# Decode attention with a cached window: V loaded and summed one quarter behind K, without filler matmuls in the loop

## The chip, the cores and the metric

The kernel runs on one core of one Trainium2 chip. The metric is the device time of one execution in microseconds (us). Three runs of the kernel before gave 291.79, 292.34 and 293.69; their median, 292.34, is the time before. A profiled execution, taken by the hardware profiler, is the source of every row quoted.

The engines are named as the profile names them: PE does the matmuls (PEld its weight loads), DVE is the vector engine, ACT the scalar engine, POOL GpSimd, and SP the engine whose queue issues nearly all DMAs.

## What is computed

One decode step of a transformer block for a batch of two, all in bfloat16:

```
h  = x + Attention(layernorm(x))        # 32 heads of 192, the last 2048 of 8192 cached tokens
h2 = h + (gelu(n @ w_gate) * (n @ w_up)) @ w_down      # n = layernorm(h)

q = (layernorm(x) @ wq)                               # x: 2 x 1 x 640
scores = q . k[window] * 192**-0.5                    # k_cache, v_cache: 2 x 32 x 8192 x 192
o = softmax(scores) . v[window];  attention = o @ wo
```

There is one query token for each of the two batch entries, so K and V are each read once and used once. They are 50 MB each (2 x 32 x 2048 x 192 x 2 bytes); with wq, wo and the three matrices of the feed-forward part it is 122 MB.

## The kernel before

**Tiles.** For each batch entry the window of 2048 tokens is cut into four *quarters* of 512 tokens. A quarter's K is one tile of 128 partitions (32 heads times 4 runs of 128 tokens) by 49152 bytes, 6.29 MB, loaded by one DMA; V likewise. So there are eight quarters, K0 to K7 and V0 to V7; quarters 0 to 3 are batch entry 0. Each quarter is worked in two *groups* `g` of 64 tokens per partition, so there are 16 groups.

**The ring.** All large loads go to one SBUF tensor, `ring`, which has three places of 49152 bytes. K tiles alternate between the first and the second (`K_AT`); V has the third alone (`V_AT`). `wq` at the start lies over the second and part of the third. After the attention, the three first parts of `wo` take the first place, the fourth part, `w_gate` and `w_up` the second, and `w_down` the third. `load` puts each DMA into a list in program order; `pump` (L358 to 374) issues from the head of that list for as long as what the next load overwrites has been marked `done`. The list is in order: a load that must wait holds back all behind it. SP issues them, and each waits there on the semaphores of the last instructions that read the place. K is marked done by its last transpose (L559), V by the second of its sums (L671).

The list is: `wq`, then K0, V0, K1, V1 to K7, V7, then four parts of `wo`, `w_gate`, two parts of `w_up`, four parts of `w_down`. A small first part of `w_gate` has a place of its own.

**One group.** `transposes(g)` (L558): 48 transposes on PE of K, seen as pairs of bfloat16 in one 4-byte word, into four half banks of PSUM, `tps`, 12 times four; each four are copied to `ktr`, 7 times by DVE (L569) and 5 times by ACT (L567). `scores(g)` (L616): 24 matmuls into the bank `sps`. `softmax(g)`: DVE masks, finds the minimum of the negated scores (L627), ACT takes the exponent into `eexp` (L631). `e_blocks(g)`: DVE transposes `eexp` into `et` (L655) and copies it in four parts (L657) into `eblk[g % 2]`, whose blocks are the weights for V. `pv(g)` (L669): 64 matmuls that sum V, weighted, into the bank `ops_` for even `g` and `m1` for odd; DVE copies the result to `osb` (L679) for three groups out of four.

**A pair of quarters.** Four groups are one turn of the loop (`J`, four turns), and the running maximum and sums are carried on once a turn: `maxima()` (DVE, ACT), `sums()` (PE, DVE, ACT), `combine()` (two pairs of small matmuls L683 and L684, then DVE: `osum` is scaled and the four partial results are added to it, L693). When a batch entry is finished, `heads_done(b)` (PE L704, DVE) arranges `osum` by heads into `ot`; for entry 0 it runs in the turn `J == 2`, for entry 1 after the loop. Then `oproj` (L728) multiplies by `wo`, and the feed-forward part follows, ending with `w_down` (L873), a cast (L879) and the store (L880).

**Fillers.** `keep_busy(n)` (L753) issues `n` matmuls of 512 columns of float32 whose result nobody reads (two instructions each). It is called with 10 ahead of the loop and with 6 after each quarter but the last.

**Order.** Each engine's order is the order in which the program calls `pe`, `dve`, `act`; `_Prog` works out the semaphore waits from what each operation reads and writes (a write to a buffer waits for its earlier readers). PE and DVE have a hardware loop of four turns; pieces that don't run in each turn (`op` for `heads_done(0)`, `fill` for the filler at the end of a turn) stand in `If` blocks, in the order given at L904. The turn of the loop is, for its two quarters:

```
transposes(g, 0, 12); scores(g); softmax(g)
transposes(g + 1, 0, 12); scores(g + 1)
e_blocks(g); softmax(g + 1)
if g % 4 == 2: maxima()
e_blocks(g + 1); pv(g)
if g % 4 == 2: sums()
pv(g + 1)
if g % 4 == 2: combine()
... heads_done(0) in turn 2, keep_busy(6)
```

Of the kernel before, what the change touches and what calls it, by code (L numbers as in the profile page):

```python
# [6 lines left out]
F32 = mybir.dt.float32  # L7
# [9 lines left out]
DH = 192  # L17
# [10 lines left out]
LOOPED = ("pe", "dve")  # L28
BIAS = 16
RARE = ()  # L30

# [24 lines left out]
class _Prog:  # L56
# [17 lines left out]
    def op(self, eng, fn, R=(), W=(), X=(), dma=None, cls=0):  # L74
        if self.seg == "op" and eng in LOOPED:
            cls = 2
        elif eng == "pe" and self.seg in RARE:
            cls = 1
# [161 lines left out]
WQ_AT = SLOT  # L240
WO_AT = (0, 15360, 30720, SLOT)
WG_AT = SLOT + 15360
WU_AT = WG_AT + 12288
WD_AT = (V_AT, V_AT + 7680, V_AT + 7680 + 3840, V_AT + 7680 + 3840 + 2560)


def bass_sequential_preLN__sliding_block_cached__geglu_ffn__decode_kernel(
# [12 lines left out]
    with ExitStack() as ctx:  # L260
# [67 lines left out]
        eblk = sb("eblk", [128, 2, 16, 4, 32], BF16)  # L328
        osb = sb("osb", [128, 4, DH], F32)
        osum = sb("osum", [128, DH], F32)  # L330
# [56 lines left out]
        def load_v(i):  # L387
            load(("v", i), V_AT, SLOT, kv_src(A_v_cache, i), lambda v: v, f"v{i % 2}")

# [49 lines left out]
        for i in range(2 * NQ):  # L439
            load_k(i)  # L440
            load_v(i)
        for J in range(4):
# [198 lines left out]
        def sums():  # L641
# [10 lines left out]
            dve(tt(wz[:, 6:7], wz[:, 5:6], zsum[:, :], ALU.mult), R=["wz5", "zsum"], W=["wz6"], cls=0)  # L652

        def e_blocks(g):
            dve(lambda e: e.transpose(et[:, :], eexp[:, :]), R=["eexp"], W=["et"], cls=0)  # L655
            for hg in range(4):
                dve(lambda e, hg=hg: e.tensor_copy(eblk[32 * hg:32 * (hg + 1), g % 2, :, hg, :],  # L657
                                                   et[32 * hg:32 * (hg + 1), :].rearrange("p (a x) -> p a x", x=32)),
                    R=["et"], W=[("eb", g % 2, hg)], cls=0)

        def pv(g):
# [14 lines left out]
            if g % 2 == 1:  # L676
                done(("v", g // 2))
            if g % 4 != 3:
                dve(lambda e: e.tensor_copy(osb[:, g % 4, :], bank[:, 0:DH]), W=[("osb", g % 4)], X=[x], cls=0)  # L679

        def combine():
            def fn(e):
                e.matmul(m2[:, 264:270], lhsT=rowperm[:, :], rhs=wz[:, 0:6], start=True, stop=True)  # L683
                return e.matmul(m2[:, 270:271], lhsT=rowsum[:, :], rhs=wz[:, 6:7], start=True, stop=True)  # L684

            pe(fn, R=["rowperm", "rowsum", "wz", "wz5", "wz6"], X=["m2"])
            dve(lambda e: e.tensor_copy(wp[:, :], m2[:, 264:270]), W=["wp"], X=["m2"], cls=0)
            dve(lambda e: e.reciprocal(rinv[:, :], m2[:, 270:271]), W=["rinv"], X=["m2"], cls=0)
            dve(tt(wfin[:, :], wp[:, 5:6], rinv[:, :], ALU.mult), R=["wp", "rinv"], W=["wfin"], cls=0)
            dve(ts(osum[:, :], osum[:, :], wp[:, 4:5], ALU.mult), R=["wp", "osum"], W=["osum"], cls=0)  # L690
            for k in range(4):
                src = osb[:, k, :] if k < 3 else m1[:, 0:DH]
                dve(lambda e, k=k, src=src: e.scalar_tensor_tensor(out=osum[:, :], in0=src, scalar=wp[:, k:k + 1], in1=osum[:, :],  # L693
                                                                   op0=ALU.mult, op1=ALU.add),
                    R=["wp", "osum"] + [("osb", k)] * (k < 3), W=["osum"], X=["m1"] * (k == 3), cls=0)

# [53 lines left out]
        def keep_busy(n):  # L750
            def fn(e):
                for k in range(n):
                    ins = e.matmul(tps[3][:, :], lhsT=identf[:, :], rhs=cf[:, :, :].rearrange("p k x -> p (k x)"), start=True, stop=True)  # L753
                return ins

            pe(fn, R=["identf", "cf0", "cfm"], X=[("t", 3)])

# [5 lines left out]
        for J in range(4):  # L763
            P.loop_seg("a", J)
            for g in (4 * J, 4 * J + 2):
# [117 lines left out]

        P.resolve({("dve", 0): 4 * 15 + 14, ("dve", 1): 0, ("dve", 2): 1, ("pe", 2): 1, ("act", 1): 0, ("act", 0): 4 * 6 + 2, ("pool", 0): 4})
        sems = {}
# [7 lines left out]
        P.emit("act", nc.scalar, sems)  # L893
        order = ["a", (1, 3, ["op"]), "b"]
        P.emit_loop("dve", nc.vector, sems, 4, order)
        P.emit_loop("pe", nc.tensor, sems, 4, order + [(None, 3, ["fill"])])

# [27 lines left out]
```

## Time and profile before

| what | value |
|---|---|
| median of three runs | 292.34 us (291.79 to 293.69) |
| the profiled execution's own time | 293.98 us |
| its span, first to last instruction | 292.7 us |
| PE busy | 220.6 us (75%), of it L558 transposes 90.4, L753 filler 50.8, L616 25.1, L669 25.8 |
| DVE busy | 149.6 us (51%) |
| ACT busy | 94.6 us (32%) |
| moved by DMA | 122.44 MB, mean 418 GB/s over the span |
| mean granted TensorE clock | 0.950 |

A row of the timeline gives the start, the length, the engine, the line, the operation and its tiles; SPq is SP's DMA queue. The row PEclk of the page, and the clock column of a windows view, give the clock that TensorE was granted as a share of full speed. Before its first recorded change, at 27.6 us, the clock is printed as 1.00 without having been recorded. Engines run beside each other, so busy times can't be added up; what sets the end is the last wait of each stage.

### The profile page before, as it was taken

What the parts mean: (1) busy time and instruction counts of PE and PEld (TensorE: products, weight loads), DVE (VectorE), ACT (ScalarE), POOL (GpSimd) and SP (SyncE); (2) the same over time, 40 slices, a digit from 0 to 9 for tenths busy, and PEclk for the clock granted to TensorE, in tenths of its full rate; (3) what the DMA queues carried; (4) which work ended last, traced back from release to release, by engine and by line L of the source; (5) the groups of instructions that cost most, each with busy time, mean ns of one, the idle gap of its engine ahead of it and who ended that gap; (6) DMA issues with size and microseconds to landing.
All of it is one profiled execution on the core that took longest, in us unless ns stands there. A gap on an engine that the chain in (4) does not pass through costs nothing.

```text
span 292.7 us, 6397 instructions
## 1 busy us (share of the span) xinstructions
PE 220.6 (75%) x2641; PEld 155.6 (53%) x2641; DVE 149.6 (51%) x369; ACT 94.6 (32%) x128; POOL 23.0 (8%) x69
## 2 busy tenths in 40 slices
PE   2008998597859795879599867988798879874974
PEld 1004476347735773477357646576657647653542
DVE  5000056715684667066834675268556844686431
ACT  1001056306530662066204640166116614550000
POOL 8930200000020000000200000000200000000000
PEclk9999999999999999999959996899799999999596
DMA  8999999999999999999999999999799999999994
GB/s 323 446 462 437 425 430 430 427 419 437 425 430 425 430 430 431 430 430 430 430 430 437 437 437 443 443 430 437 302 430 430 430 430 430 430 395 432 423 411 173
DMA packets 4203, 122.44 MB, mean 418 GB/s; under 512 B 478, under 2 KB 608, under 8 KB 1248
## 3 DMA queue, kind: packets, MB, share of 16 engines
q1 hardware_dynamic: 4188, 122.29, 97.4%
q8 instruction: 7, 0.11, 0.1%
q14 instruction: 4, 0.03, 0.0%
q10 hardware_dynamic: 4, 0.00, 0.0%
HBM read 122.29 MB, written 0.00 MB: 418 GB/s over the span
## 4 chain that ended last, share of the span: by engine, by line
DMA 40%; PE 34%; issue 9%; DVE 9%; ACT 5%; SPq 1%; DVEq 0%
DMA ring<-in_A_k_cache_dram 25%; PE tpp L558 18%; PE tpp L753 9%; DMA ring<-in_B_w_down_dram 8%; DMA ring<-in_A_wq_dram 7%; PE m L669 4%; ACT eexp L631 3%; DVE eblk L657 3%; DVE et L655 3%; PE tpp L578 2%; DVE sm L627 2%; ACT ktr L567 2%; PE sps L704 1%; PE m L683 0%; SPq L374 0%
## 5 line engine op out<-in xcount | busy, mean ns | idle before, releaser
L569 DVE COPY ktr<-tpp 128x1024 bf16<-128x1024 bf16 x112 | 76.7, 691 | 64.0 <-PE tpp L558 62.4
L567 ACT ACTIVATE ktr<-tpp 128x1024 bf16<-128x1024 bf16 x80 | 76.5, 1018 | 92.9 <-PE tpp L558 92.9
L558 PE MATMUL tpp<-identf,ring 128*128 128x128 f32 x768 | 90.4, 276 | 7.1 <-DMA ring<-in_A_k_cache_dram 4.9
L558 PEld LDWEIGHTS tpp<-identf,ring 128*128 128x128 f32 x768 | 83.1, 140 | 20.1 <-DMA ring<-in_A_k_cache_dram 7.6
L753 PE MATMUL tpp<-cf,identf 128*128 128x512 f32 x104 | 50.8, 643 | 0.0
L616 PE MATMUL sps<-ktr,rq 128*32 128x512 bf16 x384 | 25.1, 390 | 13.8 <-DVE ktr L569 13.8
L753 PEld LDWEIGHTS tpp<-cf,identf 128*128 128x128 f32 x104 | 21.1, 208 | 24.1 <-issue 23.6
L669 PE MATMUL m<-ring,eblk 128*32 128x192 bf16 x512 | 13.6, 265 | 17.1 <-DVE eblk L657 17.1
L631 ACT ACTIVATE eexp<-sm,nms 128x512 bf16<-128x512 f32 x16 | 11.6, 723 | 43.2 <-DVE nms L627 43.2
L616 PEld LDWEIGHTS sps<-ktr,rq 128*32 128x32 bf16 x384 | 9.8, 94 | 24.4 <-ACT ktr L567 17.5
L434 POOL TENSOR_TENSOR rq<-qs,mask 128x192 bf16<-128x192 bf16 x16 | 7.8, 517 | 181.8 <-PE sps L616 168.2
L669 PEld LDWEIGHTS m<-ring,eblk 128*32 128x32 bf16 x512 | 11.5, 113 | 18.3 <-DVE eblk L657 18.3
L657 DVE COPY eblk<-et 32x512 bf16<-32x512 bf16 x64 | 18.2, 285 | 2.1
L578 PE MATMUL tpp<-ring,xnT 128*32 128x384 bf16 x80 | 5.9, 482 | 15.3 <-DMA ring<-in_A_wq_dram 15.3
L627 DVE CUSTOM_DVE_ANT_1 sm<-sps,mska 128x512 f32<-128x512 f32 x16 | 11.0, 690 | 9.1 <-issue 8.8
L655 DVE STREAM_TRANSPOSE et<-eexp 128x512 bf16<-128x512 bf16 x16 | 11.3, 706 | 5.0 <-ACT eexp L631 5.0
L669 PEld LDWEIGHTS ops<-ring,eblk 128*32 128x32 bf16 x512 | 10.4, 108 | 6.1 <-DVE eblk L657 6.1
L669 PE MATMUL ops<-ring,eblk 128*32 128x192 bf16 x512 | 12.2, 248 | 1.9 <-DVE eblk L657 1.9
L578 PEld LDWEIGHTS tpp<-ring,xnT 128*32 128x32 bf16 x80 | 3.2, 137 | 17.7 <-issue 15.3
L601 DVE CAST qs<-ops 128x384 bf16<-128x384 f32 x1 | 0.6, 558 | 21.9 <-PE ops L596 21.9
L585 ACT ACTIVATE qrow<-tpp 128x768 bf16<-128x768 f32 x1 | 0.8, 811 | 20.6 <-PE tpp L578 20.6
L704 PE MATMUL sps<-onrm,colsel 128*128 128x192 f32 x8 | 3.0, 524 | 3.7 <-DVE nms L699 3.7
(143 smaller groups left out, 104.7 us busy)
## 6 DMA issues: line engine op xcount, KB each, us to landing
ring<-in_A_k_cache_dram SPq DMA_DIRECT2D x8, 6144.0 KB, 35.5
ring<-in_A_v_cache_dram SPq DMA_DIRECT2D x8, 6144.0 KB, 21.5
ring<-in_A_wq_dram SPq DMA_DIRECT2D x1, 7680.0 KB, 21.2
ring<-in_A_wo_dram SPq DMA_DIRECT2D x4, 1920.0 KB, 24.9
ring<-in_B_w_gate_dram SPq DMA_DIRECT2D x1, 1536.0 KB, 22.0
ring<-in_B_w_up_dram SPq DMA_DIRECT2D x1, 1536.0 KB, 25.3
ring<-in_B_w_down_dram SPq DMA_DIRECT2D x1, 960.0 KB, 21.6
ring<-in_B_w_down_dram SPq DMA_DIRECT2D x1, 480.0 KB, 22.4
```

The lines of the kernel that those rows point to most:

```text
L434: return lambda e: e.tensor_tensor(out=out, in0=a, in1=b, op=op)
L558: ins = e.transpose(bank[:, 128 * u:128 * (u + 1)], kv[:, off:off + 128], identf[:, :])
L567: act(lambda e, dst=dst, src=src: e.activation(out=dst, in_=src, func=ACT.Copy), W=[("kt", n)], X=[x])
L569: dve(lambda e, dst=dst, src=src: e.tensor_copy(dst, src), W=[("kt", n)], X=[x], cls=0)
L578: ins = e.matmul(tps[0][32 * r:32 * (r + 1), 0:384], lhsT=xnT[:, c, 32 * J:32 * (J + 1)], rhs=wq[:, c, 1536 * J + 384 * r:1536 * J + 384 * ...
L616: ins = e.matmul(sps[32 * hg:32 * (hg + 1), :], lhsT=rq[:, k, hg, :], rhs=cols, start=(k == 0), stop=(k == 5), tile_position=(0, 32 * hg))
L627: dve(lambda e: e.tensor_tensor_reduce(out=sm[:, :].rearrange("p (u x) -> p u x", x=32), in0=sps[:, :].rearrange("p (u x) -> p u x", x=32) ...
L631: act(lambda e: e.activation(out=eexp[:, :], in_=sm[:, :], func=ACT.Exp, bias=nms[:, n:n + 1], scale=-1.0, accum_out=zr[:, n:n + 1]), R=[( ...
L655: dve(lambda e: e.transpose(et[:, :], eexp[:, :]), R=["eexp"], W=["et"], cls=0)
L657: dve(lambda e, hg=hg: e.tensor_copy(eblk[32 * hg:32 * (hg + 1), g % 2, :, hg, :], et[32 * hg:32 * (hg + 1), :].rearrange("p (a x) -> p a ...
L669: ins = e.matmul(bank[32 * r:32 * (r + 1), 0:DH], lhsT=eblk[:, g % 2, a, :, :].rearrange("p s x -> p (s x)")[:, r:128:4], rhs=vv[:, DH * t ...
L753: ins = e.matmul(tps[3][:, :], lhsT=identf[:, :], rhs=cf[:, :, :].rearrange("p k x -> p (k x)"), start=True, stop=True)
```

## The change

The diff does five things.

1. In the list of loads, V of a quarter stands behind the next quarter's K: `wq`, K0, K1, V0, K2, V1, ... K7, V6, V7, then the weights in the same order as before.
2. V7 is loaded to the ring's first place, where K6 was. `wo`'s first three parts go to V's place and `w_down` to the first place; the rest stays.
3. The sums over a quarter's V (`pv`) are done in the next quarter, right behind that quarter's scores. For the second quarter of a pair they are in a new function `behind`, together with the scaling of `osum` and the four additions, which now read the last two partial results from PSUM; `combine` keeps the small matmuls and the weights. `behind` runs in an `If` block `pa` in the turns after the first, and once after the loop. For the first quarter of a pair they stand behind `maxima()`.
4. `e_blocks` is split: the transpose of the exponents is `e_turn`, and `e_turn(g)` stays ahead of the next softmax, while the four copies to `eblk` stand behind the sums over the earlier V, whose weights they overwrite.
5. The loop has no filler. The filler ahead of the loop has the same 10 matmuls, of 128 columns.

The diff, cut to its core:

```diff
-RARE = ()
+RARE = ("pa",)
...
-WO_AT = (0, 15360, 30720, SLOT)
+WO_AT = (V_AT, V_AT + 15360, V_AT + 30720, SLOT)
...
-WD_AT = (V_AT, V_AT + 7680, V_AT + 7680 + 3840, V_AT + 7680 + 3840 + 2560)
+WD_AT = (0, 7680, 7680 + 3840, 7680 + 3840 + 2560)
...
-            load(("v", i), V_AT, SLOT, kv_src(A_v_cache, i), lambda v: v, f"v{i % 2}")
+            load(("v", i), V_AT if i < 2 * NQ - 1 else 0, SLOT, kv_src(A_v_cache, i), lambda v: v, f"v{i % 2}")
...
             load_k(i)
-            load_v(i)
+            if i > 0:
+                load_v(i - 1)
+        load_v(2 * NQ - 1)
...
+        def e_turn(g):
+            dve(lambda e: e.transpose(et[:, :], eexp[:, :]), R=["eexp"] + [("eb", 0, 3)] * (g % 2), W=["et"], cls=0)
+
         def e_blocks(g):
-            dve(lambda e: e.transpose(et[:, :], eexp[:, :]), R=["eexp"], W=["et"], cls=0)
...
-            if g % 4 != 3:
+            if g % 4 < 2:
                 dve(lambda e: e.tensor_copy(osb[:, g % 4, :], bank[:, 0:DH]), W=[("osb", g % 4)], X=[x], cls=0)
...
+        def behind(g):
             dve(ts(osum[:, :], osum[:, :], wp[:, 4:5], ALU.mult), R=["wp", "osum"], W=["osum"], cls=0)
             for k in range(4):
-                src = osb[:, k, :] if k < 3 else m1[:, 0:DH]
+                if k == 2:
+                    pv(g)
+                    pv(g + 1)
+                src, tok, x = ((osb[:, 0, :], [("osb", 0)], []), (osb[:, 1, :], [("osb", 1)], []), (ops_[:, 0:DH], [], ["o"]),
+                               (m1[:, 0:DH], [], ["m1"]))[k]
...
-                    ins = e.matmul(tps[3][:, :], lhsT=identf[:, :], rhs=cf[:, :, :].rearrange("p k x -> p (k x)"), start=True, stop=True)
+                    ins = e.matmul(tps[3][:, 0:128], lhsT=identf[:, :], rhs=cf[:, 0, :], start=True, stop=True)
...
-                e_blocks(g)
+                e_turn(g)
                 softmax(g + 1)
-                if g % 4 == 2:
-                    maxima()
-                e_blocks(g + 1)
-                pv(g)
-                if g % 4 == 2:
-                    sums()
-                pv(g + 1)
-                if g % 4 == 2:
-                    combine()
                 if g % 4 == 0:
+                    if J > 0:
+                        P.loop_seg("pa", J)
+                        behind(g - 2)
                     if J == 2:
                         P.loop_seg("op", J)
                         heads_done(0)
+                    P.loop_seg("a2", J)
+                else:
+                    maxima()
+                    pv(g - 2)
+                    pv(g - 1)
+                e_blocks(g)
+                e_turn(g + 1)
+                e_blocks(g + 1)
+                if g % 4 == 0:
                     P.loop_seg("b", J)
-                    keep_busy(6)
-                elif J < 3:
-                    P.loop_seg("fill", J)
-                    keep_busy(6)
+                else:
+                    sums()
+                    combine()
         P.loop_seg()
+        behind(14)
         heads_done(1)
```

More of the change, by code (lines that the diff above doesn't have):

```diff
@@ L76, in op @@
             cls = 2
-        elif eng == "pe" and self.seg in RARE:
+        elif eng in LOOPED and self.seg in RARE:
             cls = 1
@@ L328, in bass_sequential_preLN__sliding_block_cached__geglu_ffn__decode_kernel @@
         eblk = sb("eblk", [128, 2, 16, 4, 32], BF16)
-        osb = sb("osb", [128, 4, DH], F32)
+        osb = sb("osb", [128, 2, DH], F32)
         osum = sb("osum", [128, DH], F32)
@@ L689, in combine @@
             dve(tt(wfin[:, :], wp[:, 5:6], rinv[:, :], ALU.mult), R=["wp", "rinv"], W=["wfin"], cls=0)
+        def behind(g):
             dve(ts(osum[:, :], osum[:, :], wp[:, 4:5], ALU.mult), R=["wp", "osum"], W=["osum"], cls=0)
             for k in range(4):
-                src = osb[:, k, :] if k < 3 else m1[:, 0:DH]
+                if k == 2:
[3 more added lines that the diff above has]
+                               (m1[:, 0:DH], [], ["m1"]))[k]
                 dve(lambda e, k=k, src=src: e.scalar_tensor_tensor(out=osum[:, :], in0=src, scalar=wp[:, k:k + 1], in1=osum[:, :],
                                                                    op0=ALU.mult, op1=ALU.add),
-                    R=["wp", "osum"] + [("osb", k)] * (k < 3), W=["osum"], X=["m1"] * (k == 3), cls=0)
+                    R=["wp", "osum"] + tok, W=["osum"], X=x, cls=0)
         def heads_done(b):
@@ L752, in fn @@
                 for k in range(n):
-                    ins = e.matmul(tps[3][:, :], lhsT=identf[:, :], rhs=cf[:, :, :].rearrange("p k x -> p (k x)"), start=True, stop=True)
+                    ins = e.matmul(tps[3][:, 0:128], lhsT=identf[:, :], rhs=cf[:, 0, :], start=True, stop=True)
                 return ins
-            pe(fn, R=["identf", "cf0", "cfm"], X=[("t", 3)])
+            pe(fn, R=["identf", "cf0"], X=[("t", 3)])
         consts_late()
@@ L881, in bass_sequential_preLN__sliding_block_cached__geglu_ffn__decode_kernel @@
              dma="dout")
-        P.resolve({("dve", 0): 4 * 15 + 14, ("dve", 1): 0, ("dve", 2): 1, ("pe", 2): 1, ("act", 1): 0, ("act", 0): 4 * 6 + 2, ("pool", 0): 4})
+        P.resolve({("dve", 0): 4 * 14 + 12, ("dve", 1): 5, ("dve", 2): 1, ("pe", 2): 1, ("act", 1): 0, ("act", 0): 4 * 6 + 2, ("pool", 0): 4})
         sems = {}
@@ L893, in bass_sequential_preLN__sliding_block_cached__geglu_ffn__decode_kernel @@
         P.emit("act", nc.scalar, sems)
-        order = ["a", (1, 3, ["op"]), "b"]
+        order = ["a", (0, None, ["pa"]), (1, 3, ["op"]), "a2", "b"]
         P.emit_loop("dve", nc.vector, sems, 4, order)
-        P.emit_loop("pe", nc.tensor, sems, 4, order + [(None, 3, ["fill"])])
+        P.emit_loop("pe", nc.tensor, sems, 4, order)
 _INS = ['A_x', 'A_k_cache', 'A_v_cache', 'A_wq', 'A_wo', 'B_x', 'B_w_gate', 'B_w_up', 'B_w_down']
```

## Prediction

> **What bounds the kernel now.** I read first the page's part 2 (40 slices of 7.3 us), because the kernel moves 122 MB:
>
> ```profile
> PEclk9999999999999999999959996899799999999596
> DMA  8999999999999999999999999999799999999994
> GB/s 323 446 462 437 425 430 430 427 419 437 425 430 425 430 430 431 430 430 430 430 430 437 437 437 443 443 430 437 302 430 430 430 430 430 430 395 432 423 411 173
> ```
>
> The transfers are busy in all slices but slice 28 (302 GB/s), the first and the last. So a change of engine work is worth only what it does to holes in this row. Second, the windows view over chosen stretches (columns: length, busy us and count of PE, PEld, DVE, ACT, POOL, granted clock, DMA share, GB/s):
>
> ```profile
> 37.85:125.41 87.56, 69.59 (x859) 49.85 (x858) 48.87 (x111) 33.80 (x44) 1.94 (x4) 1.00 1.00 433
> 125.41:210.50 85.09, 71.19 (x842) 52.96 (x846) 52.83 (x126) 34.28 (x46) 3.89 (x8) 0.91 1.00 430
> 210.50:212.50 2.00, 2.00 (x26) 1.49 (x18) 0.27 (x3) 0.00 (x0) 0.00 (x0) 0.64 0.00 0
> 212.50:256.10 43.60, 37.98 (x399) 27.55 (x398) 25.32 (x52) 18.56 (x24) 0.00 (x0) 1.00 1.01 433
> 256.10:289.78 33.68, 23.30 (x397) 14.98 (x395) 17.05 (x58) 5.40 (x11) 0.00 (x0) 0.86 0.95 398
> ```
>
> One hole of 2.00 us with nothing moved; otherwise 430 to 433 GB/s. The last stretch is the weights. Third, who made the hole: SP's queue in the timeline, which issues each V (first line) with the next K right behind:
>
> ```profile
> 178.18 0.54 SPq L374 DMA_DIRECT2D ring<-in_A_v_cache_dram  x1
> 178.76 0.60 SPq L374 DMA_DIRECT2D ring<-in_A_k_cache_dram  x1
> 211.34 0.53 SPq L374 DMA_DIRECT2D ring<-in_A_v_cache_dram  x1
> 211.92 0.61 SPq L374 DMA_DIRECT2D ring<-in_A_k_cache_dram  x1
> ```
>
> V6 went out only at 211.34, when V5 had been summed; the steps before it were 29 to 31 us, this one 33.2. Data followed 1.2 us later (212.5). Last, why it was late: the clock column, in windows of 3.41 us, on whose grid every recorded change of clock lies.
>
> ```profile
> 85.64:89.05 3.41, 1.36 (x64) 1.30 (x64) 2.73 (x12) 0.46 (x2) 0.15 (x1) 1.00 1.02 437
> 123.19:126.60 3.41, 1.55 (x12) 1.19 (x12) 0.50 (x1) 0.06 (x1) 0.00 (x0) 1.00 0.80 346
> 143.67:147.08 3.41, 1.32 (x64) 1.27 (x64) 2.73 (x12) 0.56 (x3) 0.16 (x1) 1.00 1.00 432
> 147.08:150.49 3.41, 3.41 (x20) 2.06 (x12) 1.89 (x7) 0.00 (x0) 0.00 (x0) 0.50 1.03 447
> 150.49:153.91 3.42, 3.42 (x5) 1.35 (x4) 0.42 (x1) 0.00 (x0) 0.00 (x0) 0.50 0.93 402
> 208.52:211.94 3.42, 3.40 (x68) 3.10 (x68) 0.89 (x7) 0.29 (x1) 0.00 (x0) 0.50 0.33 144
> ```
>
> After a window with PE busy 1.32 us or less the clock is 0.50 for one or two windows; after 1.36 it is not. At half clock the 12 filler matmuls took 8.05 us in place of 5.26 (chain of waits at 148.39 and 212.15), a sum over V 2.76 in place of 1.52. Fillers stand ahead of the next quarter's transposes on PE, so each such stretch delayed the following V.
>
> **The change, part by part.** A quarter is the work on one K tile (6.29 MB) in two groups. Two tiles take 29.06 us (K2 to K3, 96.35 to 125.41). Let T be a K's landing.
>
> *No filler in the loop.* 84 instructions of L753 go, seven groups of 12, at 0.43 us each 36 us of PE; they lie beside transfers, so their removal is worth only the delays above. The price: PE then sits idle from the sum over V to the next K, some 9 us, so at least one window is empty and every quarter begins at half clock. The filler ahead of the loop shrinks from 512 to 128 columns: its 20 instructions, 8.83 us, become 2.3 (at 0.116, a transpose) to 3.8 (at 0.19, its weight load). It ends by 34 and K0 lands at 38.05: quarter 0 starts cold too.
>
> *V one quarter behind.* Landings become K0 38.05, K1 52.6, V0 67.2, K2 81.7, V1, K3 and so on, 14.5 apart; bytes and their total are the same. In quarter 125.41 the scores of both groups end at 141.79, T+16.4, and two sums over V (1.52 each) now follow at once on PE, since V of the quarter before landed at T+14.5: V's place is free at T+19.5. Before, they waited for exponent, transpose and four copies, and V was free at T+22.1 (147.48). It must be free by T+29.1-1.2 = T+27.9 or the transfers run dry. So 5.8 us of room become 8.4, of which the cold start takes its part. How much: the clock came back after one full busy window at 208.52, after two at 147.08; cold lasts 3.4 to 6.8 us and costs half of that, 1.7 to 3.4, 2.6 taken. V free at T+22.1: no hole.
>
> *DVE.* The transpose of the exponents and the four copies are the same 5 instructions per group, split in two functions. Copies to osb (L679, 0.36) fall from 12 to 8: 1.4 us off DVE, off the path. The 16 multiply-adds (0.42) stay; half now read the banks of the sum directly, 0.42 too by the row that reads m. The copies to eblk now wait for the last quarter's sums over V (they reuse its place), and what is queued behind them on DVE are the next quarter's copies out of the transposes. In a first-of-pair quarter: two multiply-adds 0.84, copies 1.24, transpose 0.71, copies 1.24, about 4.1 us after V is free: T+26.2, 2.9 us ahead of the next K. In a second-of-pair quarter PE itself waits for the combine: two osb copies beside PE, then 3.2 us of copies, 1.1 of sums, 1.0 of small matmuls, 5.6 in all, T+27.7. If the room were gone, these would be added to the next quarter. In the quarter of heads_done(0) (5.2 us of DVE, 178.58 to 183.81) DVE is free at 162 + 0.8 + 5.2 + 3.3 = 171.5, K5 lands near 169: quarter 5 starts 1.6 us late (its copies begin 0.7 after its transposes), and its V is free 4 us ahead of need.
>
> *The start is tight.* Quarter 0 has no sum over V: its scores end at 54.82 in the trace, cold 56.4 to 58.2; DVE then does softmax 0.9, copies, transpose, copies, 4.2 in all, before quarter 1's first copy, so quarter 1 behaves as if K1 had landed at 59.9 to 61.7. V0 is summed at 79.4 to 81.2, and up to 3.4 later if PE's wait for DVE cools it again. V1 is wanted at 81.7-1.2 = 80.5: a hole of 0 to 4 us, 0.8 taken, since only the cooled cases reach it. K2 to K7 then have 1.4 us and more.
>
> *Places of the weights.* On SP, wo0 to wo2 now wait for V6's sum (quarter 7, about 250) while V7 runs until 256: no hole. wd waits for V7's sum, 256 + 1 to 6 us, and is wanted after wo, wg and wu, 25 us later: none either. V7 lands where it did; its sum is no longer behind quarter 7's softmax, so the head's tail starts no later. The end is what it was: last wd landed 289.78, then 0.74, 0.33, and the store to 292.7.
>
> *Branches.* One `If` more on DVE, one in place of another on PE. heads_done(0) sits in one: DVE went from 178.55 to 178.58 across it. Between 0 and 0.4 us, beside transfers: nothing.
>
> **Sum**, against the profiled execution's own time, 293.98 (span 292.7 and 1.3 around it): the hole goes, -2.0 by the empty row, -2.9 if the thin share before it (0.33 in its window: 1.1 us of work in the 4.0 from 208.52 to 212.5) counts too; I take -2.6, the fuller account less what skewed engines give back; +0.8 at V1. That is 292.2. The runs shown have a median of 292.34 and a least of 291.79, so they lost less than this execution; on their scale I take **291.9**. Its own range: 291.1 with no hole at all, less 0.3 for scatter, to 294.5 with a V1 hole of 3.5: 290.8 to 294.5.
>
> **Rivals.** *The transposes do not bring the clock back.* No row shows transposes alone doing so: it returned under filler, under q's projection, under sums over V. Half clock doubles filler (0.43 to 0.86) and makes a sum 2.76; by that, 48 transposes 5.57 become about 10.6, 24 scores 1.54 about 2.9. A quarter's scores then end at 2 x (10.6+0.9+2.9) = T+28.8, V free at T+34.3, 6.4 past need, from PE's first cold quarter on; it decides once cold lasts over 16.8 us, twice 8.4. Dense sums warm PE, and it runs on without idling, so every second quarter is spared. Quarter 0 and 1 end at 66.9 and 101.2 against 80.5: 20.7 lost, then 3 x 6.4: 291.9+40 = 332. For it: the first window at 147.08, mostly filler, did not suffice. Against: window 123.19 held only 0.36 of filler and 1.19 of transposes and did not cool where 1.32 of sums did, so transposes count almost fully. The Trainium skill's TensorE: Matmul & The Clock Gate, Part 4: PE-mode transpose, says that the full clock does not engage for transposes, which do not count as busy in the same way; by that rule this rival holds and the sum would be 332, while the trace bears it out only in that nothing shows the reverse.
>
> *It comes back only with the first scores.* Then the first group is cold (T+14.4), the second takes 8.4, V free at T+25.9: no loss in the steady state, but quarter 0 ends at 60.9, quarter 1 acts as from 64.4, and V0 is summed at 83.9 (warm) or 90.3: 3.4 to 9.8 lost, 295.3 to 301.7, say 298.
>
> *Faster.* The weights' stretch, 398 GB/s, might run at 433 with SP's waits moved: 13.4 MB in 30.9 instead of 33.7, so 291.1-2.8 = 288.3. Nothing in the change shortens these rows.
>
> **How the numbers follow.** About 1% is what a measurement can tell from no change: 289.4 to 295.3. Forecast 0.62 at 291.9; first scores 0.20, of which 0.02 stays under 295.3; no return 0.13; faster 0.05. Of the forecast 0.02 lies above 295.3. So faster 0.05, same 0.62, slower 0.33. The range, 290.3 to 302, leaves out the 332 case and the fast one, 0.18.
>
> **What would show it.** Right: slice 28's hole gone; no filler rows in the loop; granted clock 0.50 at each quarter's start and 1.00 within 7 us; SP's V issues 27 us or less after their K landings; sums of 1.52. Wrong: transposes at 0.2 us spacing for a whole group, V issues past T+28, empty DMA windows near 81 and at later tile ends. A change of the 430 GB/s itself would upset the sum altogether.

## The result and the profile after

The changed kernel is slower by 0.7%. The ratio of its runs to those of the kernel before is 1.0067 (95% interval 1.0048 to 1.0086): medians 294.63 us (22 runs, 293.62 to 298.40) and 292.31 (22 runs, 291.79 to 294.58). The time lies in the range given and within the 1% called no change, but 2.7 us above the forecast, and on the other side of the time before. Ratios here are taken over fast runs alone (three of after's 22, near 298, are left out as over 1.5% above its fastest) and are not the quotients of the medians. The profiled execution took 294.99 us with a span of 293.7, against 293.98 and 292.7.

Part 2 of the page of after, the rows that answer to those of before (40 slices of 7.34 us):

```profile
PEclk9999959979977996999599959996997599868555
DMA  8999999999889999999999999999999999999994
GB/s 322 486 425 428 424 428 428 424 418 428 353 321 428 428 430 428 428 428 442 442 455 449 428 428 428 428 442 449 428 428 428 428 428 428 428 389 430 423 416 171
```

The hole of before in slice 28 is gone (428 GB/s). A new one stands in slices 10 and 11 (353 and 321), at 73 to 88 us. The clock row shows a dip in every quarter, and a tail at half clock; 86.4 us of the span are granted half clock, in before 29.5.

SP's queue in the timeline of after, around the new hole and in the next two quarters (V first, then K):

```profile
54.55 0.54 SPq L374 DMA_DIRECT2D ring<-in_A_k_cache_dram  x1
81.34 0.54 SPq L374 DMA_DIRECT2D ring<-in_A_v_cache_dram  x1
81.92 0.60 SPq L374 DMA_DIRECT2D ring<-in_A_k_cache_dram  x1
107.89 0.54 SPq L374 DMA_DIRECT2D ring<-in_A_v_cache_dram  x1
108.47 0.61 SPq L374 DMA_DIRECT2D ring<-in_A_k_cache_dram  x1
135.04 0.54 SPq L374 DMA_DIRECT2D ring<-in_A_v_cache_dram  x1
```

The landings recorded for the issues are K0 37.87, K1 52.42, V0 67.14, K2 81.62, V1 98.86, K3 113.39. All steps are 14.5 to 14.7 us but K2 to V1, which is 17.24: a hole of 2.71. V1 was issued 0.3 us ahead of K2's landing; V2, 5.5 ahead of K3's, and V3, 7.4 ahead of K4's (142.45), left no hole, nor did any later one.

The windows view of after, half a microsecond a row (columns as before: busy PE, PEld, DVE, ACT, POOL, then clock, DMA share, GB/s):

```profile
79.50:80.00 0.50, 0.50 (x36) 0.50 (x29) 0.33 (x2) 0.50 (x1) 0.50 (x2) 1.00 0.01 0
80.00:80.50 0.50, 0.50 (x36) 0.50 (x29) 0.36 (x1) 0.45 (x3) 0.50 (x2) 1.00 0.13 33
80.50:81.00 0.50, 0.50 (x36) 0.50 (x26) 0.00 (x0) 0.00 (x0) 0.21 (x1) 1.00 0.00 0
82.00:82.50 0.50, 0.00 (x0) 0.00 (x0) 0.47 (x2) 0.00 (x0) 0.00 (x0) 1.00 0.00 0
82.50:83.00 0.50, 0.00 (x0) 0.00 (x0) 0.34 (x3) 0.00 (x0) 0.00 (x0) 1.00 2.73 885
```

This view counts a DMA packet whole in the row in which it starts (so the last row can show 2.73), and the packets of a tile are 48 KB and take 1.82 us each. What the rows say is that hardly a packet starts from 79.5 on; those begun before are still moving. Packet by packet, ten of the 16 engines ended their share of K2 between 79.52 and 79.76 and the other six by 81.16, the landing is recorded at 81.62, and V1's first packets started between 82.66 and 84.03, the first of them 1.3 us behind the issue. So the engines run dry and start again one after another. PE is meanwhile in the sums over V0 that V1 waits for. V1 landed 17.52 us behind its issue, V6 of before, in its hole, 17.50, where a tile in the flow takes 14.53. The profile of before, at the issue of V6 (211.34):

```profile
DMA to landing us min/median/max: 17.5/17.5/17.5
```

The difference of the spans is accounted for. The last tile landed at 258.70 for 257.87: 0.97 more of holes (2.88 in all for 1.91) less 0.14 for an earlier K0. The weights behind it took 32.35 us for 32.27, and from the last landing (291.05 for 290.14) to the end it was 2.63 for 2.52. That is 0.83 + 0.08 + 0.11, the 1.02 between the spans.

### The profile page after: what moved, and what is told of

Same layout as the page of the kernel before. It is cut to its first block, busy times and chain, and to the rows that moved or that the text cites. A ratio compares the mean times of both kernels' runs of the same rounds, so it can differ in the third digit from the quotient of the medians.

```text
span 293.7 us, 6215 instructions
## 1 busy us (share of the span) xinstructions
PE 188.1 (64%) x2557; PEld 155.5 (53%) x2557; DVE 148.0 (50%) x365; ACT 95.5 (33%) x128; POOL 23.0 (8%) x69
## 4 chain that ended last, share of the span: by engine, by line
DMA 56%; PE 29%; issue 6%; ACT 3%; DVE 3%; SPq 1%; DVEq 0%
DMA ring<-in_A_k_cache_dram 48%; PE tpp L560 19%; DMA ring<-in_A_wo_dram 9%; PE sps L618 3%; PE m L673 2%; PE ops L673 2%; ACT ktr L569 2%; ACT eexp L633 1%; DVE ktr L571 1%; SPq L374 1%; DVE sm L629 1%; PE sps L837 1%; PE m L886 1%; PE m L738 1%; PE ops L837 1%
## 5 line engine op out<-in xcount | busy, mean ns | idle before, releaser
L560 PE MATMUL tpp<-identf,ring 128*128 128x128 f32 x768 | 107.4, 307 | 36.6 <-DMA ring<-in_A_k_cache_dram 30.5
L560 PEld LDWEIGHTS tpp<-identf,ring 128*128 128x128 f32 x768 | 100.1, 160 | 45.6 <-DMA ring<-in_A_k_cache_dram 31.6
L569 ACT ACTIVATE ktr<-tpp 128x1024 bf16<-128x1024 bf16 x80 | 77.4, 1020 | 75.0 <-PE tpp L560 75.0
L618 PEld LDWEIGHTS sps<-ktr,rq 128*32 128x32 bf16 x384 | 10.3, 94 | 24.0 <-ACT ktr L569 17.5
L661 DVE COPY eblk<-et 32x512 bf16<-32x512 bf16 x64 | 18.2, 284 | 2.0 <-DVE nms L629 0.2
L580 PE MATMUL tpp<-ring,xnT 128*32 128x384 bf16 x80 | 5.3, 443 | 15.3 <-DMA ring<-in_A_wq_dram 15.3
L673 PE MATMUL ops<-ring,eblk 128*32 128x192 bf16 x512 | 13.7, 261 | 2.1 <-DMA ring<-in_A_v_cache_dram 2.1
L673 PEld LDWEIGHTS ops<-ring,eblk 128*32 128x32 bf16 x512 | 12.9, 112 | 3.2 <-DMA ring<-in_A_v_cache_dram 2.2
L687 PE MATMUL m<-wz,rowperm 128*128 128x6 f32 x8 | 2.4, 369 | 17.2 <-DVE wz L434 17.2
L673 PE MATMUL m<-ring,eblk 128*32 128x192 bf16 x512 | 12.7, 249 | 0.0
L580 PEld LDWEIGHTS tpp<-ring,xnT 128*32 128x32 bf16 x80 | 2.9, 127 | 17.4 <-issue 15.4
L687 PEld LDWEIGHTS m<-wz,rowperm 128*128 128x128 f32 x8 | 2.0, 312 | 17.6 <-DVE wz L434 17.6
L738 PE MATMUL m<-ring,ot 128*2 128x320 bf16 x96 | 6.3, 423 | 6.6 <-DMA ring<-in_A_wo_dram 6.6
```

Of the source, the lines that this page charges most:

```text
L560: ins = e.transpose(bank[:, 128 * u:128 * (u + 1)], kv[:, off:off + 128], identf[:, :])
L569: act(lambda e, dst=dst, src=src: e.activation(out=dst, in_=src, func=ACT.Copy), W=[("kt", n)], X=[x])
L580: ins = e.matmul(tps[0][32 * r:32 * (r + 1), 0:384], lhsT=xnT[:, c, 32 * J:32 * (J + 1)], rhs=wq[:, c, 1536 * J + 384 * r:1536 * J + 384 * ...
L618: ins = e.matmul(sps[32 * hg:32 * (hg + 1), :], lhsT=rq[:, k, hg, :], rhs=cols, start=(k == 0), stop=(k == 5), tile_position=(0, 32 * hg))
L673: ins = e.matmul(bank[32 * r:32 * (r + 1), 0:DH], lhsT=eblk[:, g % 2, a, :, :].rearrange("p s x -> p (s x)")[:, r:128:4], rhs=vv[:, DH * t ...
L738: ins = e.matmul(m1[32 * r:32 * r + 2, 192:512], lhsT=ot[:, J, kk, :], rhs=wo[:, kk, 320 * h:320 * (h + 1)], start=(J == 0 and kk == 1), s ...
```

## The experiments

Three theories of the loss stood at the outset. **A:** it all comes from V1 being late in the first turn, because quarter 0 is cold and because PE jumps over the block `pa` there. **B:** every quarter starting at half clock costs time. **C:** the cold tail does. Each kernel was timed beside the kernel before on the same chip. "Hole" is the landing of a tile less that of the one ahead of it, less 14.53. "Lead" is the landing of the K ahead less the issue of V.

What A rests on, the branch of L217 in the profile of after (first row PE's, second DVE's; the three numbers are least, median and greatest ns):

```profile
L217 PEldq COMPARE_BRANCH  x8: 65/77/4820, 55.5 to 220.5; - x8
L217 DVEq COMPARE_BRANCH  x8: 43/50/67, 57.0 to 221.2; - x8
```

and PE's timeline there, with its earlier cold quarter:

```profile
37.92 8.22 PE L560 MATMUL tpp<-identf,ring 128*128 128x128 f32 x48 [6.23 <-DMA ring<-in_A_k_cache_dram]
...
55.38 1.54 PE L618 MATMUL sps<-ktr,rq 128*32 128x512 bf16 x24 [0.86 <-DVE ktr L571]
60.64 1.76 PE L560 MATMUL tpp<-identf,ring 128*128 128x128 f32 x7 [3.72 <-issue]
```

The transposes of the first group took 8.22 us, 2.65 more than the 5.57 of before. Then one branch of eight took 4.82 us where the others took under 0.1: PE stood still for 3.72 us with K1 long there, and a 16 KB transfer of the instruction queue ran from 57.95 to 58.94, within it. Behind the standstill the clock is 0.50 from 60.52 to 63.93, so quarter 1 started cold too: its first 48 transposes took 7.13 us.

**1. The wide filler ahead of the loop again** (`e1_wide_filler_ahead`), so that quarter 0 starts warm:

```diff
-  ins = e.matmul(tps[3][:, 0:128], lhsT=identf[:, :], rhs=cf[:, 0, :], ...)
+  ins = e.matmul(tps[3][:, :], lhsT=identf[:, :], rhs=cf[:, :, :].rearrange(...), ...)
```

> The changed kernel with one part undone: the 10 fillers ahead of the loop have 512 columns again; the loop has none. Theory A (one hole in the transfers, at V1, because quarters 0 and 1 run late; its size is how late V1 is issued): quarter 0 starts at full clock, so V1 goes out about 2.1 us earlier (79.2 instead of 81.3), the hole falls from 2.7 to about 0.6, the time by 2.1, from 294.6 to about 292.5. Theory B (the half clock at the start of all eight quarters costs a little everywhere): only one of eight is warmed, gain about 0.3. Theory C (the end at half clock behind the weights' new waits): no gain.

Measured: median 293.63 (before 292.75), ratio 1.0014 [0.9984, 1.0044]. V1 was issued at 78.79, 2.55 us earlier than in after, and its hole was 1.94. The jump was still there:

```profile
L217 PEldq COMPARE_BRANCH  x8: 65/80/3740, 53.3 to 220.9; - x8
```

A cold quarter 0 is part of the loss, not all of it. And a V issued 3.2 us ahead of K2's landing is still late, which the prediction's need of 1.2 excludes.

**2. No loop: all turns written out one after another** (`e2_straight_code`), which takes away the jump:

```diff
-        P.emit_loop("dve", nc.vector, sems, 4, order)
-        P.emit_loop("pe", nc.tensor, sems, 4, order)
+        P.emit("dve", nc.vector, sems)
+        P.emit("pe", nc.tensor, sems)
```

> The changed kernel with PE's and DVE's four turns written out one behind the other, so no If and no jump; same instructions, same order. Theory A with the jump over pa in the first turn (4.8 us on PE) as one cause of V1's lateness: PE starts quarter 1's transposes some 3.7 us earlier, of which DVE, busy until 61.2 with the copies to eblk, lets 0.5 to 2.0 through; V1 goes out 0.5 to 2.0 earlier, time down by as much. If the jump is hidden by DVE: no change, 294.6. Rival: straight code is fetched late elsewhere, and new stalls of PE of several us each make it slower.

Measured: 296.75, ratio 1.0108 [1.0073, 1.0144]: slower, not faster. No branch, and V1 left 1.5 us earlier (79.8, hole 2.92, K2 having landed at 82.0). But V3, V5, V6 and V7 came 1.51, 0.69, 1.09 and 0.45 late, though they had been issued 4.9 us (V5), 8.6 (V3), 9.3 (V6) and more ahead. What is new is the code: the rows of the instruction queue in the views of DMA queues, after first, then this kernel (packets, MB):

```profile
q8 instruction: 8, 0.13, 0.2%
```

```profile
q8 instruction: 20, 0.33, 0.4%
```

Twelve more packets of 16 KB, and tiles that land late where nothing else was seen to be late. That the packets delay the tiles was not tried by itself. The same meeting is seen in the weights, whose landings are mostly 4.59 and 2.35 us apart for `wo` and the first part of `w_down`: with an instruction packet under way one was 5.49 (after, an 8 KB packet of another instruction queue at 267.8) and one 3.82 (`e6_turned_wide`, 16 KB at 282.8). But not every packet costs: in before 16 KB packets began at 77.76 and 88.76, and V1 and K2 landed on the step of 14.53.

**3. Filler in the tail** (`e4_filler_in_tail`): after, with three wide fillers behind each of the first three `oproj`.

```diff
             oproj(J)
+            if J < 3:
+                keep_busy_wide(3)
```

> The changed kernel with three wide filler matmuls behind each of the first three parts of the wo product, so that TensorE is at full clock to the end. Theory A: the last transfer's landing sets the end, so the time falls by at most 0.4 (the last matmuls behind it). Theory C: the chain from the last wo part to the store is the bound (277.98 landed, 293.7 end) and gets shorter by about 1.0 us or more.

Measured: 294.71, ratio 1.0067 [1.0033, 1.0102], what after has. The filler held the clock up from 266.5 to 287.0 (after is at 0.50 from 268.7 to the end), and the last weights landed 32.35 us behind V7, as in after. Behind the last landing, at 294.33, the clock was 0.50 again and the rest took 2.52 us, after had 2.63; so a warm end was not tried. What speaks against theory C is that the tail of before is no shorter than that either, 2.52: the tail holds 0.11 us of the loss. In this profile the jump took 8.06 us, with no edit near it, and V1 left only at 84.71, a hole of 5.52:

```profile
L217 PEldq COMPARE_BRANCH  x8: 65/84/8060, 54.5 to 224.5; - x8
```

**4. The kernel before without its loop filler** (`e5_before_no_loop_filler`):

```diff
-                    keep_busy(6)
-                elif J < 3:
-                    P.loop_seg("fill", J)
-                    keep_busy(6)
```

> The kernel before with one part of the change alone: no filler in the loop; the wide filler ahead of it, V's order and everything else as before. Theory A: V is free about T+24.7 (T+22.1 and a cold start of 2.6), wanted at T+26.1, so no hole in any quarter except perhaps behind heads_done(0): 291.9 to 292.3, no slower than before and without its executions near 293.7. Theory B: the cold starts cost, slower than before by about 2 us.

Measured: 293.72, ratio 1.0022 [0.9989, 1.0054], unclear in sign. Its profile (span 291.9, clock 0.91 for 0.95) has no V hole; K1 was 0.59 late. No loss of the filler alone is shown, but an interval up to 0.54% does not exclude most of after's 0.67% either.

**5 and 6. The loop turned** so that no turn jumps ahead of PE's work on K1: the scores of groups 0 and 1 stand ahead of the loop, a turn ends with the next pair's first scores and its sums over V, in blocks that only the last turn skips. `e7_turned_loop` has the narrow filler of after, `e6_turned_wide` the wide one.

```diff
+        front(0)
         for J in range(4):
...
+            if J < 3:
+                P.loop_seg("an", J)
+                front(g + 4)
+                P.loop_seg("pa", J)
+                behind(g + 2)
...
-        order = ["a", (0, None, ["pa"]), (1, 3, ["op"]), "a2", "b"]
+        order = ["a2", (None, 3, ["an", "pa"]), (0, 2, ["op"])]
```

> The changed kernel with the loop turned: scores and softmax of quarter 0 stand ahead of it, and a turn ends with the next first quarter's scores, behind and heads_done(0), in an If that only the last turn skips. Same instructions, same order, no skipped code in the first turn; the filler ahead of the loop stays narrow. The jump theory: PE starts quarter 1's transposes right behind quarter 0's scores (57 in place of 60.6), V1 goes out at about 79.8 as in the straight code, but without its extra code fetches; its hole then is 2 or less in place of 2.7, and executions near 296 and 298 (longer jumps) vanish: about 293.7. If the jump costs nothing because DVE holds PE up anyway: 294.6, unchanged.

> The turned loop and the 10 wide fillers ahead of it, so both causes of V1's lateness are gone. Theory A (all of the loss is the one hole at V1): V1 goes out at about 77.5, over 4 us ahead of K2's landing, no hole; 291.9 to 292.3, the same as before or a little faster. Theory B (cold quarters cost everywhere): at most 0.5 better than the wide filler alone, 293.2 or more.

Measured: `e7_turned_loop` 293.86 (before 292.45), ratio 1.0065 [1.0038, 1.0092]; `e6_turned_wide` 292.81, ratio 1.0013 [0.9990, 1.0036]. In the first the longest branch is 233 ns:

```profile
L217 PEldq COMPARE_BRANCH  x4: 68/75/233, 104.3 to 255.6; - x4
```

The issues of V1, `e7_turned_loop` and then `e6_turned_wide`:

```profile
79.28 0.54 SPq L374 DMA_DIRECT2D ring<-in_A_v_cache_dram  x1
```

```profile
76.79 0.53 SPq L374 DMA_DIRECT2D ring<-in_A_v_cache_dram  x1
```

In these four profiles the two causes add up: 81.34 in after; 78.79 with the wide filler; 79.28 with the turn, 2.06 earlier; 76.79 with both, 4.55 earlier, 2.55 + 2.06 within 0.1. That it fits so closely is partly luck: a second profile with both (section 9) has 78.50. The jump of 4.82 us and the cold start behind it are worth only 2.06, since DVE was busy with its copies to `eblk` until 61.2 anyway. With both edits the slices from 73 to 88 us are full, as the GB/s row of `e6_turned_wide` shows, and K2 to V1 is 14.56 us:

```profile
GB/s 324 439 472 438 427 431 431 427 426 427 427 431 427 432 428 431 431 431 431 431 431 431 431 431 431 431 431 431 431 431 431 431 431 431 415 430 417 426 412 111
```

After's loss is gone with the hole as far as the interval tells (it leaves up to 0.36%), as A has it, though the quarters from the third on still start at half clock (first at 82.06) and the mean clock is 0.875.

**7. All old fillers back, at the old width** (`e8_filler_back_in_loop`): after's order of V and K, with the filler of before.

```diff
+                    keep_busy(6)
...
+                    if J < 3:
+                        P.loop_seg("fill", J)
+                        keep_busy(6)
```

> The changed kernel with all of the old filler back (10 wide ones ahead, 6 behind each quarter but the last), V one quarter behind as in the change. Theory A: the filler keeps TensorE at full clock but the start is still late by the jump or by the filler standing in its place (5.3 us between quarter 0 and 1): V1 goes out at 78 to 80, hole 1 to 2.5, time 292.5 to 294, no better than the wide filler alone. Theory B (cold quarters cost everywhere): clearly faster than the wide filler alone, 292 or less.

Measured: 299.20 (six runs), ratio 1.0184 [1.0136, 1.0232]. It is the slower kernel by far, yet it does not decide on B, since its start is worse. In its profile PE jumps for 5.82 us and only then runs the filler, which by then is cold (12 matmuls, 7.67 us), ahead of quarter 1:

```profile
L217 PEldq COMPARE_BRANCH  x8: 65/84/5820, 52.9 to 228.5; - x8
```

V1 left at 85.57, 3.79 behind K2's landing, for a hole of 6.76, and V2 left one of 1.73. Theory B falls by after itself: each of its quarters starts at half clock, and no tile behind V1 was late.

**8. One more load ahead** (`e9_turned_wide_wg0`): `e6_turned_wide` with the small first part of `w_gate` loaded behind K2, not ahead of the loop.

```diff
-        load_wg0()
         load_wq()
...
+        load_wg0()
```

> The turned loop with wide filler, and the small first part of w_gate (0.39 MB, 0.9 us of transfer) loaded behind K2 in place of ahead of everything. K0 to K2 land 0.9 us earlier and the small load stands between K2 and V1, so V1 is wanted no earlier while quarters 0 and 1 end 0.9 earlier. Theory A: no hole if one was left in the turned loop with wide filler, else the same time: 291.7 to 292.3.

Measured: 293.00, ratio 1.0024 [1.0009, 1.0039]. V1 left at 77.6, 3.7 ahead of K2's landing, and landed 1.42 late; 0.93 of that is the small load, which lands between the two. No gain.

With these and the next profiles, the lead and the hole of a V can be set side by side, each from one profile:

| kernel | lead, us | hole, us |
|---|---|---|
| e8_filler_back_in_loop, V1 | -3.79 | 6.76 |
| e4_filler_in_tail, V1 | -2.64 | 5.52 |
| after, V1 | 0.28 | 2.71 |
| e8_filler_back_in_loop, V2 | 1.19 | 1.73 |
| before, V6 | 1.22 | 1.75 |
| e2_straight_code, V1 | 2.20 | 2.92 |
| e7_turned_loop, V1 | 2.75 | 1.92 |
| e1_wide_filler_ahead, V1 | 3.23 | 1.94 |
| e12_turned_wide_again, V1 | 3.48 | 1.99 |
| e11_code_on_pool, V1 | 4.26 | 1.96 |
| before, V7 | 4.26 | 0.00 |
| e4_filler_in_tail, V2 | 4.79 | 0.01 |
| e6_turned_wide, V1 | 5.04 | 0.03 |

In the first five rows lead and hole add up to 2.9 to 3.0: each us late costs a whole us, and the need is 3.0, the 17.5 from issue to landing of a V that finds the engines dry less the 14.53 of one in the flow. The next five rows are 1.7 to 2.2 worse than that. In each of those profiles one of the 16 engines began its share of V1 only 3.2 to 3.8 us behind the issue, where the first began 1.3 behind it, and a 16 KB instruction packet had started 0.3 to 1.3 us ahead of V1's first packet (at 79.28 to 79.83). In `e6_turned_wide` such a packet started at 79.60, 2.8 us behind V1's issue, and cost nothing. That the packet held that engine back fits, and is not shown: the trace doesn't say which engine it ran on, and no run moves it.

**9. The turned kernel again** (`e12_turned_wide_again`, the same code as `e6_turned_wide`), beside the next two:

> The turned loop with wide filler once more, as the base for the next one on the same chip: no hole at V1, 292.3 to 293.0.

Measured: 292.75 (before 292.62), ratio 0.9993 [0.9968, 1.0019]. Together with the first time: the turned kernel with the wide filler is as fast as the kernel before, no faster. In this profile V1 left at 78.5 with a hole of 1.99: the last 32 transposes of quarter 1's first group took 5.38 us for 3.80 in the other profile of the same code, since the clock was 0.50 from 60.17 to 63.58, where the other stayed at 1.00. The profiled execution, 293.67, is the slowest of the twelve.

**10. Code on an idle engine** (`e11_code_on_pool`): `e6_turned_wide` with 400 one-element memsets on POOL behind each `rq` multiplication, 1600 in all, into a tile that nothing reads. It was meant to bring in instruction packets without touching PE or DVE.

```diff
+            for _ in range(400):
+                n = len(P.per["pool"]) % 1600
+                P.per["pool"].append(_Op("pool", 0, lambda e, n=n: e.memset(idle[:, n:n + 1], 0.0)))
```

> The turned loop with wide filler, and 1600 one-element memsets on POOL (400 behind each masking of q; about 100 KB of code, 0.1 us each) into a tile that nothing reads; POOL is idle there, so only the code fetches are new. Theory of the fetches (each 16 KB fetch takes about 1 us of one of the 16 DMA engines and holds the tile in flight up by as much): some six fetches more, single tiles landing 0.5 to 1.5 us late without their issue being late, 1 to 6 us slower in all. Rival (fetches are hidden, late landings in the straight code came from late issues): same time within 0.3.

Measured: 302.35, ratio 1.031 [1.0254, 1.0367]. But it doesn't tell what it was meant to tell. DVE's timeline, first this kernel, then `e6_turned_wide`, the same four copies and the four after them:

```profile
78.70 7.00 DVE L665 COPY eblk<-et 32x512 bf16<-32x512 bf16 x4
85.83 0.71 DVE L661 STREAM_TRANSPOSE et<-eexp 128x512 bf16<-128x512 bf16 x1
86.57 3.91 DVE L665 COPY eblk<-et 32x512 bf16<-32x512 bf16 x4
```

```profile
77.07 1.22 DVE L661 COPY eblk<-et 32x512 bf16<-32x512 bf16 x4
78.42 0.71 DVE L657 STREAM_TRANSPOSE et<-eexp 128x512 bf16<-128x512 bf16 x1
79.17 1.23 DVE L661 COPY eblk<-et 32x512 bf16<-32x512 bf16 x4
```

While POOL ran its memsets (77.71 to 92.7, with two pauses) four of DVE's copies together took up to six times as long, and the transpose between them not a bit longer. All 64 copies rose from 18.2 to 43.2 us. Quarter 2 then began at 92.13 in place of 81.87, and V2, issued 31.2 us behind K2's landing, left a hole of 3.31. The cost of instruction packets by themselves stays open. The Trainium skill, GPSIMD Engine Reference, section Specifications, says that GpSimd shares its SBUF interfaces with VectorE and contends with some of its instructions, those in a two-port mode or with two SBUF inputs; these rows agree in that some of DVE's instructions are slowed and others not.

**11. The kernel before with half its loop filler** (`e10_before_short_filler`):

```diff
-                    keep_busy(6)
+                    keep_busy(3)
...
-                    keep_busy(6)
+                    keep_busy(3)
```

> The kernel before with 3 wide fillers behind each quarter in place of 6. Theory A (fillers at half clock made V6 late in some executions): filler of 2.6 us, or 5.2 at half clock, no longer reaches past the next K's landing, so the executions near 293.7 go and the fastest stay: median 291.8 to 292.1, 0.1 to 0.2% under before. If the clock falls more often instead: 292 to 293, as without filler in the loop.

Measured: 292.03 (before 292.62), ratio 0.9969 [0.9940, 0.9998]. It is the one version whose interval lies below the kernel before, by 0.3%, and it only just leaves out no change. Its one profile shows V6 issued at 207.19, 4.15 us earlier than in before, with K6 landing at 212.7, and no slice like slice 28:

```profile
GB/s 324 413 492 432 427 439 432 429 421 432 434 432 427 405 432 440 432 432 432 432 432 432 432 432 432 432 432 432 432 432 432 432 432 432 406 422 432 423 412 131
```

In that profile the one hole of before is gone with two numbers changed, where the change studied rebuilt the loop for it.

## Why the prediction named the holes and had the sign wrong

**The need of V1, the step that failed most.** "It must be free by T+29.1-1.2 = T+27.9", and in the start, "V1 is wanted at 81.7-1.2 = 80.5: a hole of 0 to 4 us, 0.8 taken". K2 landed at 81.62 as foretold, the sum over V0 ended at 81.30 (foretold: 79.4 to 81.2, or later if PE cooled again), and V1 left at 81.34, 0.8 past 80.5. That the time of V1 fit is partly luck: without the jump, which the prediction put at nothing, it left at 79.28 (`e7_turned_loop`). But the hole was 2.71. The 1.2 is the time from the issue to the first data. It was set against the landing of the tile ahead, which is that of its last part, while the engines run dry one after another ahead of it and start again one after another. The trace of before had the true price: V6 went out at 211.34 and K6 landed at 212.56, 1.2 later, so by that rule nothing should have been lost there, yet V6 landed 17.50 behind its issue. Less 14.53 that is a need of 3.0, so V1 was wanted at 78.6, not at 80.5. The size taken was within the bounds of 0 to 4, and the error is 1.9 us of it. (The prediction's row from 210.50 to 212.50, "with nothing moved", counts packets where they start; the last of K6 was under way until 212.13.)

**The hole of V6.** "The hole goes, -2.0 by the empty row ... I take -2.6". By landings it was 1.75 in the profiled execution. Against the median there was less to gain: 293.98 - 1.75 = 292.23, close to the median of the 22 runs (292.31). So about half the runs of before seem to have no such hole; only one execution of before was profiled, so this is argued from the times and not shown. The prediction said that the runs lost less than the profiled execution, and then moved by only 0.3 for it.

With 2.71 in place of 0.8 and 1.75 in place of 2.6, the profiled execution would have been put at 293.98 - 1.75 + 2.71 = 294.94; it was 294.99. And from a median without the hole, 292.3 + 2.7 = 295.0 against the 294.63 measured.

**Branches.** "Between 0 and 0.4 us, beside transfers: nothing." The block `pa` is jumped over in the first turn. That took 4.82 us on PE, and 3.74, 5.82 and 8.06 in three other profiles; with the cold start behind it, it was worth 2.06 us of V1's lateness. The rows read for it in before were DVE's, around a block in the third turn. In all four profiles one 16 KB instruction packet lies inside the jump, and the jump ends 1.36 to 1.37 us behind the end of that packet, whatever its length: 57.07 behind 55.71 (e1), 60.30 behind 58.94 (after), 58.69 behind 57.32 (e8), 62.58 behind 61.22 (e4). So the jump waited for that packet, as far as four traces without an edit to it can show; why the packet came when it did stays open.

**The clock.** What was forecast of the quarters held. Four windows of 3.41 us of after, on the grid of its clock changes, across the start of quarter 3 (the clock is the third number from the end):

```profile
108.30:111.71 3.41, 0.00 (x0) 0.00 (x0) 2.87 (x9) 0.00 (x0) 0.00 (x0) 1.00 1.07 461
111.71:115.12 3.41, 1.68 (x8) 1.69 (x9) 0.53 (x1) 0.00 (x0) 0.00 (x0) 0.50 1.07 461
115.12:118.53 3.41, 3.41 (x18) 3.41 (x17) 1.38 (x3) 2.05 (x2) 0.00 (x0) 0.50 1.06 461
118.53:121.94 3.41, 2.92 (x26) 2.58 (x24) 2.69 (x5) 2.66 (x3) 0.00 (x0) 1.00 0.90 389
```

After a window without PE the clock is 0.50. K3 landed at 113.39, and all that PE ran from 113.44 to 121 was L560. After one window full of transposes the clock is back, 5.1 us behind their start. So the first rival, 332 us, is refuted: transposes do bring the clock back. The rule of the Trainium skill, TensorE: Matmul & The Clock Gate, Part 4: PE-mode transpose, by which it would have held, does not agree with these rows, at least not for these transposes (`e.transpose` on PE, 4-byte words). The second rival, that only the scores bring it, falls by the same rows. The later V went out 20.7 to 21.7 us behind the landing of their quarter's K (V3 at 135.04 for 113.39), near the 19.5 warm and 22.1 cold foretold; V2 at 26.3, its quarter being held up by the late V1; none left a hole. The prediction's bound for cooling (1.32 us of PE in a window or less, not 1.36) is not general: the window 265.31:268.73 of after, with PE busy 1.50 us, most of it in the product with `wo`, was followed by half clock.

**Weights, DVE, the end.** As foretold: `wo` was issued from 251.2 on while V7 landed at 258.70, the first part of `w_down` at 263.13, 25 us ahead of its landing; `wo`'s steps are 4.59 or 4.60 with one of 5.49, in before 4.56 to 4.69. The tail is at half clock from 268.7 and still ends 2.63 us behind the last landing. The third rival, weights at 433 GB/s, did not come: 32.35 us for 32.27.

**What stays open.** The turned kernel has no V hole in the first of its two profiles, yet no run of it was below 292.38, where before has runs at 291.5 on the same chip. Its two profiles show something late each time (3.82 for 2.35 us at `w_down`; the V1 hole of 1.99), each with an instruction packet beside it. Whether those packets are the rest could not be told, since the experiment for it slowed DVE.

## What to carry to other kernels

When a queue of large transfers must not run dry, the lead that an issue needs is not the time to its first data. Take it from a transfer that did find the engines dry: its time from issue to landing less the step of one in the flow, here 17.5 - 14.5 = 3.0 us. Leads of 2.2 to 4.3 were not always enough. Look at the first turn of a loop by itself, because a block skipped there is a jump over code that has not yet run, here 3.7 to 8.1 us. And before rebuilding a loop to remove a hole, compare the profiled time with the median of the runs: what the median does not hold can't be gained.

## What the runs showed of the hardware that was not expected

- A branch of PE over a block not run before took 3.74, 4.82, 5.82 and 8.06 us in four profiles, and ended 1.36 to 1.37 us behind the end of a 16 KB instruction packet each time; the others there took 0.07 to 0.23.
- Instruction packets of 16 KB travel beside the tiles, 7 to 9 in a kernel with loops and 20 without; some landings with one under way came 1.5 to 2 us late (`w_down` in e6, V1 in e12), others, as V1 and K2 of before, not at all.
- A 6.29 MB tile issued to engines that had run dry landed 17.4 to 17.5 us behind its issue (e4, before, after, e8), with its first packet 1.3 behind it; one in the flow took 14.53. The 16 engines ended the tile ahead 1.6 and 2.1 us apart (after, before).
- Memsets of one element on POOL stretched DVE's bf16 copies from 0.28 to 0.68 us on average and left its transposes at 0.70 to 0.71.
